# Fused chunk attention and snake MLP: k and q of batch 1 as fp32 through SyncE's queue, whole-width transposes, and a new order of work

## The chip, the cores and the metric

The kernel runs on one NeuronCore of a Trainium2 chip. TensorE (PE), VectorE (DVE), ScalarE (ACT), GpSimd (POOL) and SyncE (SP) each work off their own instruction stream in order. They meet at semaphores. DMAs are issued from SP and ACT on one kind of queue and from POOL on another. The metric is the device time of one execution in microseconds; the median of three runs is compared.

## The reference

Four batches of 768 tokens, eight heads of 64. Each chunk of 32 queries attends to 8 memory keys and to its own 32 keys with 16 to the left and 8 to the right; the result, 3072 x 512, goes through a two-layer network with a sine between.

```python
for c in range(nc):                                  # chunks of 32 queries
    l_start, r_end = max(0, c_start - 16), min(S, c_end + 8)
    k_full = concatenate([mem_k, k[:, :, l_start:r_end]], axis=2)
    v_full = concatenate([mem_v, v[:, :, l_start:r_end]], axis=2)
    a = softmax(scale * q_c @ k_full.T)
    out[:, :, c_start:c_end] = a @ v_full
x = out.transpose(0, 2, 1, 3).reshape(B * S, H * D)
h = x @ w_in                                         # 512 -> 2048
s = sin(alpha * h)
g = h + s * s / (alpha + 1e-09)
return g @ w_out                                     # 2048 -> 512
```

## The kernel before, in words

The work goes batch by batch. A front (a `Stage` with index -1) does the attention of batch 0. Then four passes follow. Pass i does both layers of batch i and, inside it, the attention of batch i + 1, so that PE has something to do while the other engines work on a tile.

**Attention.** Queries are taken 96 at a time. Scores need k and q with the head dimension on the partitions. Batches 0 and 1 get them by PE: `turn` (L269) transposes one piece, that is two heads (a head pair, `hp`) of k or of q, in twelve transposes of 128 x 64, and `put_k` (L282) or `put_q` (L297) copies the result out of PSUM. Batches 2 and 3 use DMA transposes. `scores` and `u_scores` take the exponential on ACT. `values` and `u_values` multiply with v and, in `normed` (L350), divide by the row sums on DVE. `turned` (L362) turns the result on PE and writes it to `xT`.

**Where k and q come from.** Batch 0: eight loads of 384 KB in fp32 by SP (`load_f`, L707) into `kq_f`, cast on chip piece by piece (L653, word "a"). Batch 1: two loads of 768 KB by POOL (`load_one`, L154, words "dq108" and "dk108"), which cast on the way, so no engine casts. Batches 2 and 3: rows by POOL (L232, L238, L245).

**The network.** For each of 16 tiles of the hidden layer (`ft`): `half_tile` (L422) does two halves of four matmuls with 384 columns; `sine` (L435) on ACT; `squared` (L441) on ACT, DVE or POOL, as a letter says; `finish` (L449) on DVE writes `gT`. The second layer (`second`, L458) has 96 matmuls of 512 columns a batch, which `feed` gives out in portions.

**The order is written out by hand.** Strings of words are read from left to right, and each word issues instructions. "b4" and "h4" are the two halves of tile 4, "q4V" its square on DVE, "g4" its end; "k0" and "l0" transpose the pieces of k and q for head pair 0, "K0V" and "L0A" copy them out on DVE and ACT; "a0V" casts piece 0 (0 to 3 are k, 4 to 7 q); "s", "v", "t"/"T"/"c" are scores, values and turns; "f7" gives out seven second-layer matmuls. Words that issue POOL DMAs: "V024" loads v of batch 0, heads 2 and 3 (`load_v`, L160, two DMAs, three for the first heads); "I02" loads `w_in` for tiles 0 and 1 (`load_w_in`, L212); "U56" loads `w_out` for tile 5; "dm" loads the memory values. "C" words make constants: "Cp", "Cz", "Cv", "Cs" and "Ci" on POOL. Each engine keeps the order of the words for its own instructions, POOL's DMA issues included, and waits where data is late.

In the front, POOL's order before is: Cp, Cz, Cv, Ci, dm, V024, V002, V068, V046, Cs, I02, I27; then from pass 0 I7g, U69, U12, dq108, dk108, Ufg, U01, U56. The first tile of batch 0 is b0, which needs I02 and the first half of `xT`.

Of the kernel before, what the change touches and what calls it, by code (L numbers as in the profile page):

```python
# [85 lines left out]
def kernel(  # L86
# [182 lines left out]
    def turn(src, hp):  # L269
        bank, bs = banks.single()  # L270
        t = bank[:, 0:384].bitcast(BF).rearrange("p (r c) -> p r c", r=6)
        for r in range(6):
            for e in range(2):
                nc.tensor.transpose(
                    t[64 * e:64 * e + 64, r, :], src[:, 2 * hp + e, r, :], ident[:]
                )
# [226 lines left out]
    class Stage:  # L503
# [146 lines left out]
        def do_a(self, a):  # L650
            hp = int(a[0]) % HP
            dst = kq[int(a[0]) // HP]
            copier(a[1])(  # L653
                dst[:, 2 * hp:2 * hp + 2].rearrange("p h r d -> p h (r d)"), kq_f[int(a[0])][:]
            )
# [7 lines left out]
        def do_d(self, a):  # L663
            if a == "m":
                nc.gpsimd.dma_start(memv_st[64:72].rearrange("n b h d -> n (b h) d"),
                                    mem_v.rearrange("b h n d -> n (b h) d"))
# [206 lines left out]
```

## Time and profile before

| What | Value |
|---|---|
| Median of three runs | 216.53 us (216.51 to 219.29) |
| Profiled execution: span from first to last instruction | 213.1 us |
| Median less span | 3.4 us |
| PE busy | 201.7 us, 95% of the span |
| ACT, DVE, POOL busy | 143.5, 140.5, 99.8 us |
| First of the 512 first-layer matmuls | 24.81 us |
| Granted clock of TensorE | 1.000 |

No time of its own is listed for the profiled execution beside the span, so the median less the span stands in for what lies around it. In the rows below, a row by stretches gives the stretch, its length, then busy time and instructions of each engine, the granted clock, the DMA share and GB/s. A row by time gives start, duration, engine, line, operation, tiles, shape and count; in brackets stands how long the engine sat idle before, and what ended that. A row of a DMA queue gives packets, MB and the share of 16 engines, which can pass 100% as packets overlap. A DMA's row gives issuer, count, size and microseconds from issue to landing.

### The profile page before, as it was taken

Reading aid. Unit: us, or ns where it says so; the run is one execution under the profiler, and the core shown is the slowest. Engines: PE = TensorE matmul, PEld = TensorE weight load, DVE = VectorE, ACT = ScalarE, POOL = GpSimd, SP = SyncE. Lnnn points to the kernel's source line nnn. Section 1 sums busy time; section 2 is a strip of 40 time slices with the busy share of each in tenths; the row PEclk is TensorE's granted clock in tenths of the full one; section 3 lists DMA queues with packets and bytes.
Section 4 is the critical chain, followed back from the end, with each engine's and each line's share of the span. In section 5 each row is a group of like instructions: output and inputs, shape, how many; then the busy total and the mean of one; then the engine's idle time right before and its main releaser. Section 6 shows DMA issues by size and latency. Waiting matters only on the chain.

```text
span 213.1 us, 4479 instructions
## 1 busy us (share of the span) xinstructions
PE 201.7 (95%) x1721; PEld 113.5 (53%) x1721; DVE 140.5 (66%) x218; ACT 143.5 (67%) x230; POOL 99.8 (47%) x140
## 2 busy tenths in 40 slices
PE   0799899999999999999999999999999999999994
PEld 0456555565455556555455555554555555554443
DVE  7598678999542749975856649898157197865011
ACT  2597898976857469977846199887846289891110
POOL 8959515688598193009991039659400023200000
PEclk9999999999999999999999999999999999999999
DMA  6999999999999999969999229989945400000312
GB/s 195 337 163 141 193 209 205 204 163 182 131 177 141 137 148 144 180 88 110 126 217 171 72 63 131 156 126 129 175 115 123 124 15 0 2 3 0 148 49 98
DMA packets 95908, 28.19 MB, mean 132 GB/s; under 512 B 84864, under 2 KB 92432, under 8 KB 95888
## 3 DMA queue, kind: packets, MB, share of 16 engines
q0 software_dynamic: 68736, 13.25, 92.3%
q1 hardware_dynamic: 26976, 14.62, 28.2%
q8 instruction: 13, 0.21, 0.4%
q14 instruction: 7, 0.06, 0.1%
q10 hardware_dynamic: 176, 0.04, 0.1%
HBM read 29.66 MB, written 6.29 MB: 169 GB/s over the span
## 4 chain that ended last, share of the span: by engine, by line
PE 71%; DVE 9%; DMA 7%; ACT 4%; issue 4%; POOL 3%; DVEq 0%; POOLq 0%; ACTq 0%
PE ps L462 38%; PE ps L424 27%; DMA memv_st<-in_mem_v_dram 4%; DVE gT L451 4%; DVE s L447 3%; DMA vw<-in_v_dram 3%; PE ps L414 3%; PE ps L385 2%; ACT u L439 2%; PE ps L366 1%; ACT s L444 1%; POOL s L447 1%; POOL vw L172 1%; DVE kT L285 1%; ACT L699 1%
## 5 line engine op out<-in xcount | busy, mean ns | idle before, releaser
L462 PE MATMUL ps<-w_out_sb,gT 128*128 128x512 bf16 (+2 forms) x400 | 89.1, 371 | 0.0
L424 PE MATMUL ps<-xT,w_in_sb 128*128 128x384 bf16 x512 | 86.0, 326 | 0.7 <-DVE gT L451 0.4
L451 DVE SCALAR_TENSOR_TENSOR gT<-s,inv_alpha,ps 128x768 bf16<-128x768 f32 x64 | 63.0, 1011 | 12.5 <-ACT s L444 5.2
L424 PEld LDWEIGHTS <-w_in_sb 128*128 128x128 bf16 x512 | 49.8, 98 | 35.4 <-issue 2.1
L439 ACT ACTIVATE u<-ps,alpha_sb 128x768 f32<-128x768 f32 x64 | 56.6, 895 | 16.8 <-PE ps L424 14.3
L462 PEld LDWEIGHTS <-gT 128*128 128x128 bf16 x400 | 36.6, 98 | 37.9 <-DVE gT L451 0.2
L447 POOL TENSOR_TENSOR s<-u 128x768 f32<-128x768 f32 x11 | 17.4, 1582 | 69.7 <-ACT u L439 69.7
L399 ACT ACTIVATE pt<-ps,biasm 128x256 bf16<-128x256 f32 x72 | 27.2, 489 | 10.5 <-PE ps L385 10.5
L469 DVE COPY o_sb<-ps 128x512 f32<-128x512 f32 (+1 forms) x15 | 10.1, 678 | 28.3 <-PE ps L462 26.4
L447 DVE TENSOR_TENSOR s<-u 128x768 f32<-128x768 f32 x23 | 21.9, 953 | 7.8 <-ACT u L439 7.8
L444 ACT ACTIVATE s<-u 128x768 f32<-128x768 f32 x30 | 25.0, 841 | 0.5
L354 DVE TENSOR_TENSOR x_blk<-ps,rinv 96x512 bf16<-96x512 f32 x32 | 22.0, 687 | 1.1
L469 ACT COPY o_sb<-ps 128x512 f32<-128x512 f32 (+1 forms) x10 | 5.6, 562 | 21.6 <-PE ps L462 21.6
L172 POOL DMA_DIRECT2D vw<-in_v_dram x13 | 12.9, 994 | 7.9 <-PE ps L366 5.4
L353 DVE RECIPROCAL rinv<-ps 96x8 f32<-96x8 f32 x32 | 6.4, 200 | 13.5 <-PE ps L414 12.7
L179 POOL DMA_DIRECT2D vw<-in_v_dram x13 | 12.7, 976 | 0.0
L238 POOL DMA_DIRECT2D kst<-in_k_dram x16 | 12.2, 760 | 1.1 <-DMA vw<-in_v_dram 0.8
L232 POOL DMA_DIRECT2D kst<-in_k_dram x16 | 11.3, 708 | 2.3 <-DMA vw<-in_v_dram 1.6
L369 ACT COPY xT<-ps 128x384 bf16<-128x384 bf16 x12 | 5.6, 496 | 8.2 <-PE ps L366 8.2
L245 POOL DMA_DIRECT2D q_bf<-in_q_dram x12 | 10.7, 912 | 0.0
L414 PEld LDWEIGHTS <-pt 128*128 128x128 bf16 x192 | 8.2, 97 | 4.2 <-ACT pt L399 0.3
L414 PE MATMUL ps<-vw,pt 128*128 128x65 bf16 x192 | 8.9, 193 | 0.0
(81 smaller groups left out, 131.4 us busy)
## 6 DMA issues: line engine op xcount, KB each, us to landing
out_dram<-o_sb SPq DMA_DIRECT2D x23, 256.0 KB, 2.3
kq_f<-in_k_dram SPq DMA_DIRECT2D x4, 384.0 KB, 6.5
kq_f<-in_q_dram SPq DMA_DIRECT2D x4, 384.0 KB, 6.0
q_bf<-in_q_dram POOLq DMA_DIRECT2D x12, 128.0 KB, 6.7
w_in_sb<-in_moe_w_in_dram POOLq DMA_DIRECT2D x1, 1152.0 KB, 12.6
vw<-in_v_dram POOLq DMA_DIRECT2D x7, 128.0 KB, 6.7
vw<-in_v_dram POOLq DMA_DIRECT2D x8, 112.0 KB, 7.4
kst<-in_k_dram POOLq DMA_DIRECT2D x14, 64.0 KB, 5.1
```

The lines of the kernel that those rows point to most:

```text
L172: nc.gpsimd.dma_start(vw[0:64, lo:c1, 0:D], win(vflat, a, n, 64))
L179: nc.gpsimd.dma_start(vw[72:128, c0:hi, 0:D], win(vflat, base + QW * c0 + 48, hi - c0, 56))
L354: nc.vector.tensor_tensor(out=x_blk[:].rearrange("p g e d -> p e g d"), in0=otv[0:QW, :, :, 0:D], in1=rinv[:].unsqueeze(3).to_broadcast([Q ...
L399: nc.scalar.activation(pt[:, 0:H * QW].rearrange("p (g e c) -> p g e c", g=2, e=4)[:, :, :, 32 * m:32 * m + 32], sc[:, :, 0:4 * QW].rearra ...
L414: nc.tensor.matmul(otv[:, e, hp, :], pt[:, QW * i:QW * i + P], vws[b % 2][:, 2 * hp + e, j, 0:D + 1],)
L424: nc.tensor.matmul(t["hT"][:, hf, 0:HALF], w_in_sb[:, kt, P * t["ft"]:P * t["ft"] + P], t["xT"][:, kt, HALF * hf:HALF * hf + HALF], start= ...
L439: nc.scalar.activation(t["u"][:], t["hT"][:, :, 0:HALF], ACTF.Sin, scale=alpha_sb[:, ft:ft + 1])
L444: nc.scalar.activation(s2[:], u[:], ACTF.Square)
L447: e.tensor_tensor(out=s2[:], in0=u[:], in1=u[:], op=ALU.mult)
L451: nc.vector.scalar_tensor_tensor(out=gT[:, ft, :].rearrange("p (e c) -> p e c", e=2), in0=t["s2"][:], scalar=inv_alpha[:, ft:ft + 1], in1= ...
L462: nc.tensor.matmul(o[:, c0:c1], gT[:, ft, P * s:P * s + P], w_out_sb[:, ft, c0:c1], start=(ft == 0), stop=(ft == FT - 1),)
L469: copier(state["engines"][state["o"] % len(state["engines"])])(o_sb[:, c0:c1], o[:, c0:c1])
```

## The change

1. The two POOL loads of k and q for batch 1 go. Instead SP loads eight fp32 pieces of 384 KB into a new buffer `kq_1` (word "j": "jkP0123" and "jqP0123" in pass 0). A small memset on POOL stands ahead of each four; the loads wait for it. `kq_1` takes one of the two buffers of `gT`.
2. Eight casts for batch 1 in pass 0: "a7P", "a6P", "a0P", "a1P" on POOL, "a4V", "a2V", "a3V" on DVE, "a5A" on ACT. The casts of batch 0 may stand on POOL too: "a0P" and "a2P" in the front.
3. The casts write the two heads of a piece side by side, so that `turn` needs six transposes of 128 x 128 instead of twelve of 128 x 64.
4. All five strings are new. In the front POOL's order becomes: Ci, a0P, Cz, dm, Cv, V002, a2P, V024, V046, Cp, V068, Cs, I27, I02; then in pass 0 I7g, the memset for k, U69, U12, U01, U24, Ufg, the memset for q, the square of tile 6, that of tile 7, a6P, a7P, U56, U45. The second-layer portions are mostly smaller ("f16" becomes "f12 f1" and the like); there are 96 matmuls a batch as before.

```diff
+FRONT = (
+    'Cb a1A Ci Cm a4V a0P k0 a5A z4 l0 Cz K0V Cl We dm Cv k1 V002 Ck L0A l1 K1A a3V L1A a6A a7V a2P s00 '
+    's01 k2 l2 m0 K2A s10 V024 V046 eVA s11 z4 k3 Cp L2V v10 l3 V068 K3A L3A Cs I27 s20 v11 v01 s30 v00 '
+    'z1 s31 v30 s21 T01 v31 T10 v20 T00 eVA T30 v21 z1 T31 z1 t20 t11 I02 t21 Ws '
+)
+PASSES = ((
+    'o8 b0 I7g jkP0123 h0 b1 U69 h1 U12 b4 q0V q1A g0 h4 b3 h3 g1 q4V q3A g4 U01 b6 b2 h2 U24 Ufg h6 b5 '
+    'h5 jqP0123 g3 b7 q6P q2V h7 q7P a6P q5A g2 a7P U56 a4V b10 g6 g5 h10 b9 q10A h9 b8 h8 g7 q8A g10 q9V '
+    'a2V b11 h11 g9 b13 g8 U45 h13 l0 q11V l2 l3 k2 a0P L0A L2A V158 q13A g11 g13 K2A a1P b15 h15 Uef '
+    'q15V b12 Ube g15 h12 q12A U9b a5A b14 V102 V125 g12 h14 q14P f7 k0 k1 l1 a3V L3A k3 K1V L1V K3A f4 '
+    'f1 f3 f2 f3 K0A s61 g14 f12 f1 s70 f1 f8 s3 f1 f1 m1 v6 v0 f1 f1 f1 f7 v3 f3 f2 t0 f1 s542 f1 f5 f4 '
+    'T3 f1 v1 f1 f1 f2 v4 v2 f2 f3 Ws c4 v7 f1 c6 c2 f1 t1 f1 f1 v5 f2 f3 f4 f1 T7 f2 f1 f1 T5 f5 '
...
-    k_bf = consts.tile([P, H, 6, D], BF, name="k_bf")
-    q_bf = consts.tile([P, H, 6, D], BF, name="q_bf")
+    k_bf = consts.tile([P, HP, 6, 2, D], BF, name="k_bf")
+    q_bf = consts.tile([P, HP, 6, 2, D], BF, name="q_bf")
...
-    def load_one(src, dst, b, h0, h1):
-        nc.gpsimd.dma_start(
-            dst[:, h0:h1].rearrange("p h r d -> p h (r d)"),
-            src[b, h0:h1].rearrange("h (p r) d -> p h (r d)", p=P),
-        )
...
         for r in range(6):
-            for e in range(2):
-                nc.tensor.transpose(
-                    t[64 * e:64 * e + 64, r, :], src[:, 2 * hp + e, r, :], ident[:]
-                )
+            nc.tensor.transpose(
+                t[:, r, :], src[:, hp, r].rearrange("p e d -> p (e d)"), ident[:]
+            )
...
-            copier(a[1])(
-                dst[:, 2 * hp:2 * hp + 2].rearrange("p h r d -> p h (r d)"), kq_f[int(a[0])][:]
-            )
+            copy = nc.gpsimd.tensor_copy if a[1] == "P" else copier(a[1])
+            copy(dst[:, hp].rearrange("p r e d -> p e r d"),
+                 kq_f[int(a[0])].rearrange("p e (r d) -> p e r d", r=6))
...
+        def do_j(self, a):
+            x0 = 0 if a[0] == "k" else HP
+            hps = [int(c) for c in a[2:]]
+            eng = {"V": nc.vector, "P": nc.gpsimd}[a[1]]
+            for hp in hps:
+                kq_f[x0 + hp] = kq_1[:, x0 + hp]
+            eng.memset(kq_1[0:1, x0 + hps[0]:x0 + hps[-1] + 1, 0, 0:1], 0.0)
+            for hp in hps:
+                load_f(k if x0 == 0 else q, hp, kq_f[x0 + hp], 1)
...
+    kq_1 = gp.tile([P, 2 * HP, 2, 6 * D], F32, name="kq_1", tag="gT")
...
-    stage.run((
-        'a1A Cb Cp Cz Cv a5A eVA Cm Cl z4 a0V Ci k0 dm a4V l0 k1 K0V Ck l1 L0A V024 We L1V a2A K1A V002 '
-        'a6V k2 s00 K2V a3V s11 V068 m0 a7V s01 l2 s10 k3 K3A L2A V046 z4 v10 l3 Cs L3A I02 v11 s20 z1 '
-        'v01 s30 z1 v00 s31 z1 v30 s21 v31 T01 T10 v20 T30 T00 v21 T20 T31 I27 t11 t21 eVA Ws '
-    ))
-    for i, words in enumerate(((
-        'o8 b0 h0 I7g q0V U69 U12 b1 h1 dq108 q1A b4 h4 b3 g0 h3 b6 g1 dk108 q4V g4 q3A b2 h2 h6 b5 h5 '
-        'Ufg g3 b7 q2V U01 U56 q6P h7 g2 q5A b10 U24 q7P g6 h10 b9 q10A g5 h9 U45 b8 h8 g7 g10 q8A q9V '
-        'V158 b11 h11 g9 b13 g8 h13 l0 l2 l3 L0A L2A q13P k2 q11V Ube b15 U9b g11 Uef g13 K2V h15 b12 '
-        'q15V h12 q12A b14 g15 f7 h14 V125 k1 k0 g12 l1 K1V k3 L1V L3A q14V K3A K0A V102 f9 g14 s61 f16 '
-        'm1 s70 s3 f13 v0 f3 v6 c6 f6 v3 f5 s542 T3 f10 T0 v4 f6 v2 f2 v1 c4 c2 f7 v7 f1 T1 f3 v5 Ws T7 '
-        'f8 t5 '
...
+    stage.run(FRONT)
+    for i, words in enumerate(PASSES):
```

The strings of passes 1 to 3 are new in the same manner: the same tiles, squares, scores, values and loads in another order, with smaller portions.

More of the change, by code (lines that the diff above doesn't have):

```diff
@@ L18 @@
 ALU = mybir.AluOpType
+FRONT = (
[3 rows of a table added]
+)
+PASSES = ((
[6 rows of a table added]
+), (
[5 rows of a table added]
+), (
[5 rows of a table added]
+), (
[3 rows of a table added]
+))
 class Feed:
@@ L138 @@
     kst = consts.tile([P, NJ, H * D], BF, name="kst")
-    k_bf = consts.tile([P, H, 6, D], BF, name="k_bf")
-    q_bf = consts.tile([P, H, 6, D], BF, name="q_bf")
-    qst = q_bf[:].rearrange("p h r d -> p (h r d)").rearrange("p (t c) -> p t c", t=NSUB)
+    k_bf = consts.tile([P, HP, 6, 2, D], BF, name="k_bf")
+    q_bf = consts.tile([P, HP, 6, 2, D], BF, name="q_bf")
+    qst = q_bf[:].rearrange("p g r e d -> p (g r e d)").rearrange("p (t c) -> p t c", t=NSUB)
     NK = NM * sum(not CROSSED[b][0] for b in range(B))
@@ L672, in do_d @@
                             mem_k[bb].rearrange("h n d -> n h d"))
-            else:
-                src, dst = (k, k_bf) if a[0] == "k" else (q, q_bf)
-                load_one(src, dst, int(a[1]), int(a[2]), int(a[3]))
+        def do_j(self, a):
[7 more added lines that the diff above has]
+                load_f(k if x0 == 0 else q, hp, kq_f[x0 + hp], 1)
         def do_I(self, a):
@@ L699, in warm, with load_f @@
         nc.scalar.activation(tiny[:], zeros[0:1, 0:1], func)
-    kq_f = [mlp.tile([P, 2, 6 * D], F32, name="kq_f", tag=t) for t in ("u", "s2") * 4]
+    kq_f = [mlp.tile([P, 2, 6 * D], F32, name="kq_f", tag=t)[:] for t in ("u", "s2") * 4]
+    kq_1 = gp.tile([P, 2 * HP, 2, 6 * D], F32, name="kq_1", tag="gT")
     memk_f = mlp.tile([P, H, D], F32, name="memk_f", tag="o_sb", bufs=3)
     alpha_rows = mlp.tile([FT, P], F32, name="alpha_rows", tag="o_sb", bufs=3)
-    def load_f(src, hp, t):
+    def load_f(src, hp, t, b=0):
         nc.sync.dma_start(
-            t[:], src[0, 2 * hp:2 * hp + 2].rearrange("h (p r) d -> p h (r d)", p=P)
+            t, src[b, 2 * hp:2 * hp + 2].rearrange("h (p r) d -> p h (r d)", p=P)
         )
@@ L812 @@
     stage.tile = first
-    stage.run((
[3 rows of a table removed]
-    ))
-    for i, words in enumerate(((
[6 rows of a table removed]
-    ),(
[5 rows of a table removed]
-    ),(
[5 rows of a table removed]
-    ),(
[3 rows of a table removed]
-    ))):
+    stage.run(FRONT)
+    for i, words in enumerate(PASSES):
         stage = Stage(i, stage.nx).run(words)
```

26 rows, old and new, of tables (PASSES, stage) are left out of this document.

## The prediction

> **What bounds the kernel now.** I read the page's totals first, then the busy time by stretches, then the front in order of time, then the DMA queues by window.
>
> ```profile
> span 213.1 us, 4479 instructions
> PE 201.7 (95%) x1721; PEld 113.5 (53%) x1721; DVE 140.5 (66%) x218; ACT 143.5 (67%) x230; POOL 99.8 (47%) x140
> ```
> ```profile
> 24.00:28.00 4.00, 3.85 (x36) 2.47 (x33) 1.87 (x4) 3.51 (x6) 1.03 (x2) 1.00 1.14 213
> 28.00:36.00 8.00, 7.83 (x48) 4.48 (x46) 7.01 (x9) 6.86 (x9) 1.82 (x2) 1.00 1.21 206
> 36.00:44.00 8.00, 7.99 (x88) 5.14 (x87) 7.49 (x8) 7.85 (x11) 5.17 (x6) 1.00 1.28 205
> 44.00:54.00 10.00, 9.69 (x105) 5.50 (x106) 9.54 (x14) 6.86 (x10) 9.08 (x12) 1.00 1.91 166
> 190.00:213.10 23.10, 20.24 (x110) 9.96 (x108) 5.67 (x7) 4.10 (x7) 0.00 (x0) 1.00 0.18 69
> 28.00:213.10 185.10, 181.36 (x1414) 100.13 (x1411) 119.87 (x163) 124.84 (x203) 78.24 (x89) 1.00 1.13 121
> ```
> The first number after the length is PE's busy time, then PEld, DVE, ACT, POOL. From 28 us to the end PE lacks 185.1 - 181.4 = 3.7 us, of which 23.1 - 20.2 = 2.9 us is the tail behind its last matmul. So between 28 us and the tail only 0.8 us is idle. Two things set the time: the moment at which the first-layer matmuls of batch 0 begin, and the amount of PE work behind it. The span stands 3.4 us under the median of the runs (216.5); I add every change to that median.
>
> The front decides the first of the two:
>
> ```profile
> 4.86 0.90 POOL L665 DMA_DIRECT2D memv_st<-in_mem_v_dram  x1
> 6.57 1.12 POOL L179 DMA_DIRECT2D vw<-in_v_dram  x1
> 14.34 1.76 POOL L172 DMA_DIRECT2D vw<-in_v_dram  x1 [2.52 <-DMA memv_st<-in_mem_v_dram]
> 16.09 0.88 POOL L179 DMA_DIRECT2D vw<-in_v_dram  x1
> 18.03 2.27 POOL L213 DMA_DIRECT2D w_in_sb<-in_moe_w_in_dram  x3
> 27.01 0.54 POOL L219 DMA_DIRECT2D w_out_sb<-in_moe_w_out_dram  x1 [2.52 <-DMA w_in_sb<-in_moe_w_in_dram]
> ```
> ```profile
> 16.11 0.41 PE L344 MATMUL ps<-vw,pt 128*128 128x65 bf16 x8
> 22.29 0.42 PE L344 MATMUL ps<-vw,pt 128*128 128x65 bf16 x8 [0.25 <-DMA vw<-in_v_dram]
> 24.81 17.62 PE L424 MATMUL ps<-xT,w_in_sb 128*128 128x384 bf16 x104
> ```
> ```profile
> w_in_sb<-in_moe_w_in_dram POOLq DMA_DIRECT2D x1, 256.0 KB, 4.6
> w_in_sb<-in_moe_w_in_dram POOLq DMA_DIRECT2D x1, 640.0 KB, 7.9
> ```
> Two waits of POOL show a rule of its queue. The ninth DMA (14.34) waited for the first to land, the twentieth (27.01) for the twelfth, the 640 KB of w_in: eight are in flight. The two w_in pieces landed at 18.03 + 4.6 = 22.6 and at 27.0, in the order of issue. The first value matmuls went at 16.1 and the last v load released PE at 22.3: six full-sized v loads and one tiny one in 6.2 us, about 1 us each. POOL's queue works its loads off one behind the other, and the first layer, at 24.8, followed close on them.
>
> **The change part by part.**
>
> *The w_in pieces change places.* In the new front "I27" (640 KB, columns of first-layer tiles 2 to 6) stands ahead of "I02" (256 KB, tiles 0 and 1), and the first tile is still b0. The columns of b0 now land behind everything that had landed at 27.0 before: the same v loads and the same two pieces. POOL also has a cast, "a0P", ahead of its first load; it waits for k's first piece. So the memory load goes out near 6 us, not at 4.9. That costs little, since POOL's queue moved nothing so early anyhow:
>
> ```profile
> q1 hardware_dynamic: 909, 1.32, 100.1%
> ```
> ```profile
> q1 hardware_dynamic: 198, 0.29, 95.3%
> q0 software_dynamic: 195, 0.01, 25.0%
> ```
> ```profile
> q0 software_dynamic: 560, 0.78, 114.0%
> ```
> ```profile
> q0 software_dynamic: 4318, 0.52, 369.6%
> ```
> ```profile
> q0 software_dynamic: 787, 0.09, 72.5%
> q1 hardware_dynamic: 249, 0.45, 64.2%
> ```
> These are the queues (packets, MB, share) in five windows: 5 to 9 us, SyncE's queue alone; 10 to 11, both; 22 to 26, POOL's queue alone with w_in; 14 to 18, the same with v; 59 to 61, both, with k rows and stores. In the first the two quoted loads of POOL were out, and none of their packets moved. So the floor for b0 is 27.0, against 24.8: +2.2 us.
>
> *K and q of batch 1 go to SyncE's queue.* POOL loses two issues and gains a tiny memset, behind its third w_in issue; eight loads of 384 KB then follow on SP, four at that memset and four at a second one. I estimate when, from POOL's rows and k's first load:
>
> ```profile
> kq_f<-in_k_dram SPq DMA_DIRECT2D x1, 384.0 KB, 3.9
> ```
> That load, issued in the first microsecond, takes 3.9 to land, so the cast ends near 5.5; the memory load and seven v issues of about 0.9, the second POOL cast and the memsets bring POOL to some 15, the last two v issues to 17, two memsets to 18, and three w_in issues in 2.27 to 20.1; SyncE's first bytes follow near 21.5. At that time the last w_in data are still to come. Taking some 2 us from data to landing (a store of the page's list lands in 2.3), data ran until 25.0: 3.5 us of POOL's queue are left at 21.5. A packet takes 16 engines x 4 us / 909 = 70 ns on SyncE's queue, 16 x 4 / 560 = 114 ns for w_in. Dealt one for one, as the equal counts of 10 to 11 us say (198 and 195), POOL's queue keeps 114 / 184 = 62%: 3.5 / 0.62 = 5.6 us, so b0's columns land at 21.5 + 5.6 + 2.0 = 29.1. The bounds are 27.0 (no contention) and, with POOL's queue at the 35% of its bytes that 59 to 61 shows (0.09 / 2 = 0.045 MB/us, where v alone moves 0.52 / 4 = 0.13), 21.5 + 10 + 2 = 33.5. I take 29.0, since w_in has long packets, and those of 59 to 61 are short. The Trainium skill, "DMA: Bandwidth & Descriptors", section "Queues, rings and completion order", says that each DMA engine goes round robin between its queues, a whole packet at a time. By that rule the landing is the 29.1 of the sum, by the byte shares 33.5; the equal counts at 10 to 11 us agree with it, 787 to 249 at 59 to 61 does not, and 909 to none at 5 to 9 does not either.
>
> *The value chain of the front.* The loads of heads 6 and 7 are now the last; four value groups need or follow them, where two did. Each has a reciprocal and a scaling on DVE:
>
> ```profile
> L354 DVE TENSOR_TENSOR x_blk<-ps,rinv 96x512 bf16<-96x512 f32 x32 | 22.0, 687 | 1.1
> L353 DVE RECIPROCAL rinv<-ps 96x8 f32<-96x8 f32 x32 | 6.4, 200 | 13.5 <-PE ps L414 12.7
> ```
> Two more at 0.89 put the first layer at 24.8 + 1.8 = 26.6, under the 29.0 of the weights: hidden by that wait, and worth 1.8 us if it were gone. The casts and transposes that come earlier in the front are hidden by the v loads: at nothing, with 16.1 as their due time.
>
> *Six transposes a piece.* Twelve halves become six whole ones.
>
> ```profile
> 42.30:44.00 1.70, 1.63 (x48) 1.45 (x48) 1.00 1.23 202
> 49.60:51.20 1.60, 1.52 (x48) 1.37 (x48) 1.00 1.27 212
> ```
> ```profile
> L462 PE MATMUL ps<-w_out_sb,gT 128*128 128x128 bf16 x16 | 1.1, 219 | 0.0
> ```
> Batch 1's 96 take 1.63 + 1.52 = 3.15 us, 33 ns each: halves already overlap in pairs. A whole one has 128 columns at full width. By the first-layer row 17.62 / 104 = 169 ns for 384 columns, so 56 ns; by the row above 1.1 / 16 = 69 ns. 48 of them cost 2.7 to 3.3 us: between 0.45 less and 0.15 more. I take 0.4 less, as back to back is the nearer case. In batch 0 it lies ahead of the v loads and counts nothing.
>
> *Eight casts more.* Four on POOL, three on DVE, one on ACT.
>
> ```profile
> L653 DVE CAST q_bf<-kq_f 128x768 bf16<-128x768 f32 x3 | 2.2, 728 | 0.0
> L653 ACT CAST q_bf<-kq_f 128x768 bf16<-128x768 f32 x1 | 0.8, 832 | 0.2 <-DMA kq_f<-in_q_dram 0.2
> L760 POOL COPY mind<-asum 128x768 bf16<-128x768 bf16 x1 | 0.8, 815 | 0.0
> L447 DVE TENSOR_TENSOR s<-u 128x768 f32<-128x768 f32 x23 | 21.9, 953 | 7.8 <-ACT u L439 7.8
> L444 ACT ACTIVATE s<-u 128x768 f32<-128x768 f32 x30 | 25.0, 841 | 0.5
> L285 DVE COPY kT<-ps 128x672 bf16<-128x672 bf16 x4 | 3.4, 853 | 0.9 <-PE ps L274 0.9
> ```
> DVE gains 3 x 0.73 and gives away one square (0.95) and one k copy (0.85): +0.4. ACT gains the cast (0.83), that square (0.84) and that copy (at its cast's rate 0.83 at most): +2.5. In the stretch 28 to 54 DVE is busy 7.01 + 7.49 + 9.54 = 24.0 of 26 us and ACT 21.6; ACT's rises to 24.1. Both still fit, so I take nothing; with no slack the two would cost at most 2.9. POOL's four (0.82 each, bounded above by the time for which q is late) stand ahead of w_out issues; see the rivals.
>
> *Order and smaller portions in batches 1 to 3.* PE has 0.8 us to win in all, so I take 0.2 off. The cover is second-layer work; where it ran out, at least a tile's sine and square would be exposed, 0.9 + 0.95 us at a time:
>
> ```profile
> L439 ACT ACTIVATE u<-ps,alpha_sb 128x768 f32<-128x768 f32 x64 | 56.6, 895 | 16.8 <-PE ps L424 14.3
> ```
>
> Sum: 216.5 + 4.2 - 0.4 - 0.2 = **220.1 us**.
>
> **The rivals.**
> 1. *POOL's queue is crowded out.* With the 35% above, b0 begins at 33.5: 216.5 + 8.7 - 0.6 = 224.6. The blank POOL queue at 5 to 9 us speaks for it, the long packets of w_in against. It makes the kernel over 2% slower as soon as b0 begins later than 24.8 + 4.3 + 0.6 = 29.7.
> 2. *POOL blocks on q.* "a6P" and "a7P" wait on POOL for the last q pieces. Eight pieces of 384 KB (3.1 MB) at 38% of SyncE's 1.32 / 4 = 0.33 MB/us take up to 25 us, until 46, and the w_out issues of tiles 4 and 5 stand behind them on POOL. The second layer starts here before the change:
>
> ```profile
> 47.43 1.67 PE L462 MATMUL ps<-w_out_sb,gT 128*128 128x512 bf16 x7
> ```
> It would be due near 47.4 + 4.2 = 51.6. If q lands after 48, these loads stop PE; at 50 it costs some 2: 222.1.
> 3. *No contention.* SyncE's loads come later or POOL's keep their rate: b0 at 27.0, 218.1.
> 4. *Faster.* b0's columns do not hang on the 640 KB (the pieces travel side by side) and the value chain closes as early as before: 24.8, and PE wins 0.4 and the 0.8 idle: 215.3. Against it stand the landings in the order of issue. Over 2% faster would need b0 before 22, ahead of the last v load.
>
> **How the numbers follow.** Forecast 43% (218.8 to 221.2), rival 1 17%, rival 2 10%, rival 3 20%, rival 4 10%. Two per cent, about what a measurement of this kernel tells from no change, is 4.3 us: 212.2 to 220.9. Slower: all of rival 1, nearly all of rival 2, and about 0.13 of the forecast, whose upper end passes 220.9: 39%. Faster: 4%, from the far end of rival 4. The same: 57%. The range leaves out the lower part of rival 4 and the upper part of rival 1: 216.2 to 224.2.
>
> **What would show it.** In the changed profile, the first L424 matmul near 29 and waiting on w_in; the 256 KB load landing behind the 640 KB one; SyncE's eight 384 KB loads beside w_in from 21.5; 48 transposes near 2.75 us; PE full from there to the tail. The prediction is wrong if the first layer starts by 25, if PE waits for a cast, or if PE has new gaps of over 1 us behind 54 us.

## The result and the profile after

The changed kernel takes 233.84 us (median; 233.25 to 235.8), the kernel before 216.52 beside it: a ratio of 1.0835, interval [1.0769, 1.0902]. 220.1 was forecast. Times here are medians of all executions, while ratios leave out disturbed ones (over 1.5% above the fastest of the same kernel), as are the profiles of E1, E12 and E15 and all of E1's times but 227.8 us.

The page of the changed kernel: the span, PE's row, and the two lines of the chain that ended last.

```profile
span 231.6 us, 4322 instructions
PE 206.8 (89%) x1625; PEld 115.5 (50%) x1625; DVE 142.1 (61%) x219; ACT 144.3 (62%) x230; POOL 103.1 (45%) x147
...
PE 49%; DMA 21%; POOL 10%; ACT 7%; issue 6%; DVE 6%; SPq 1%; DVEq 0%; ACTq 0%
PE ps L484 29%; PE ps L446 15%; DMA kq<-in_q_dram 8%; ACT u L461 5%; DMA q_bf<-in_q_dram 4%; DVE gT L473 3%; DMA kT<-kst 3%; PE ps L436 2%; DMA xT<-x_blk 2%; POOL vw L202 2%; PE ps L407 2%; POOL vw L195 2%; DMA kq_f<-in_k_dram 2%; DVE s L469 2%; POOL w_out_sb L242 1%
```

Three things that the prediction's sum did not price stand in the chain: the new q loads (8%), the row loads of q in the later batches (4%) and the DMA transposes of k (3%). To place them I cut both spans at the first first-layer matmul of each pass. First the kernel before, then the changed one; columns as in the prediction's rows by stretches (stretch, length, PE, PEld, DVE, ACT, POOL, granted clock, DMA, GB/s).

```profile
24.81:75.48 50.67, 50.17 (x472) 28.57 (x470) 35.52 (x52) 38.23 (x63) 30.66 (x38) 1.00 1.60 174
75.48:122.06 46.58, 46.57 (x376) 25.71 (x374) 33.48 (x48) 32.60 (x57) 22.30 (x27) 1.00 1.56 139
122.06:168.14 46.08, 45.92 (x357) 25.00 (x355) 30.04 (x42) 34.04 (x57) 21.37 (x23) 1.00 1.16 122
168.14:213.10 44.96, 41.88 (x241) 22.80 (x239) 21.88 (x24) 22.83 (x30) 4.44 (x3) 1.00 0.13 48
```
```profile
28.56:83.82 55.26, 51.90 (x420) 29.12 (x421) 37.27 (x53) 38.80 (x63) 35.13 (x43) 0.97 1.43 170
83.82:133.40 49.58, 47.28 (x372) 25.92 (x372) 34.13 (x48) 31.42 (x56) 19.51 (x24) 1.00 1.26 128
133.40:184.76 51.36, 47.43 (x357) 25.45 (x354) 28.98 (x41) 35.21 (x58) 21.20 (x24) 0.97 1.11 108
184.76:231.60 46.84, 42.23 (x241) 22.62 (x239) 23.61 (x25) 21.27 (x28) 6.09 (x4) 1.00 0.14 49
```

| | before | after | difference | of it PE idle |
|---|---|---|---|---|
| first first-layer matmul | 24.81 | 28.56 | +3.75 | |
| pass 0 | 50.67 | 55.26 | +4.6 | +2.9 |
| pass 1 | 46.58 | 49.58 | +3.0 | +2.3 |
| pass 2 | 46.08 | 51.36 | +5.3 | +3.8 |
| pass 3 | 44.96 | 46.84 | +1.9 | +1.5 |

PE idle is length less busy. In passes 0 and 2 the rest is busy time too long, and the clock column says why: 0.97. The front costs about what was forecast. The other 14.7 us lie where the forecast had 0.6 to win.

The front and pass 0 on PE, and the two other engines that matter there:

```profile
28.56 10.71 PE L446 MATMUL ps<-xT,w_in_sb 128*128 128x384 bf16 x64 [2.18 <-DMA w_in_sb<-in_moe_w_in_dram]
...
43.14 7.04 PE L446 MATMUL ps<-xT,w_in_sb 128*128 128x384 bf16 x32 [2.26 <-DVE gT L473]
...
55.80 1.67 PE L484 MATMUL ps<-w_out_sb,gT 128*128 128x512 bf16 x7
```
```profile
40.75 1.41 DVE L676 CAST q_bf<-kq 128x768 bf16<-128x768 f32 x1 [1.39 <-DMA kq<-in_q_dram]
42.08 3.77 DVE L473 SCALAR_TENSOR_TENSOR gT<-s,inv_alpha,ps 128x768 bf16<-128x768 f32 x4
```
```profile
45.50 0.82 POOL L676 CAST q_bf<-kq 128x768 bf16<-128x768 f32 x1 [3.76 <-DMA kq<-in_q_dram]
46.86 1.08 POOL L676 CAST q_bf<-kq 128x768 bf16<-128x768 f32 x1 [0.53 <-DMA kq<-in_q_dram]
47.89 1.14 POOL L242 DMA_DIRECT2D w_out_sb<-in_moe_w_out_dram  x2
```
```profile
44.00:48.00 4.00, 4.00 (x17) 1.95 (x15) 3.56 (x5) 1.24 (x2) 1.96 (x3) 0.61 0.25 84
```
The first layer waits for w_in, as forecast. Then DVE reaches its cast of q's first piece (word "a4V") before the piece is there, waits 1.39 us and takes 1.41 for it. Four "finish" steps queue behind it; they free the PSUM banks that PE needs, and PE stands 2.26 us. For the next 4 us the granted clock is 0.61, and 17 matmuls take the 4.00 us in which 24 of 169 ns would fit. POOL waits 3.76 us for another piece of q, and the next w_out issue goes out at 47.89.

### The profile page after: what moved, and what is told of

Its sections match the earlier page's. It is cut to its first block, busy times and chain, and to the rows that moved or that the text cites. A ratio compares the mean times of both kernels' runs of the same rounds, so it can differ in the third digit from the quotient of the medians.

```text
span 231.6 us, 4322 instructions
## 1 busy us (share of the span) xinstructions
PE 206.8 (89%) x1625; PEld 115.5 (50%) x1625; DVE 142.1 (61%) x219; ACT 144.3 (62%) x230; POOL 103.1 (45%) x147
## 4 chain that ended last, share of the span: by engine, by line
PE 49%; DMA 21%; POOL 10%; ACT 7%; issue 6%; DVE 6%; SPq 1%; DVEq 0%; ACTq 0%
PE ps L484 29%; PE ps L446 15%; DMA kq<-in_q_dram 8%; ACT u L461 5%; DMA q_bf<-in_q_dram 4%; DVE gT L473 3%; DMA kT<-kst 3%; PE ps L436 2%; DMA xT<-x_blk 2%; POOL vw L202 2%; PE ps L407 2%; POOL vw L195 2%; DMA kq_f<-in_k_dram 2%; DVE s L469 2%; POOL w_out_sb L242 1%
## 5 line engine op out<-in xcount | busy, mean ns | idle before, releaser
L446 PE MATMUL ps<-xT,w_in_sb 128*128 128x384 bf16 x512 | 87.7, 330 | 7.0 <-DVE gT L473 2.4
L484 PE MATMUL ps<-w_out_sb,gT 128*128 128x512 bf16 (+2 forms) x400 | 91.4, 374 | 0.4 <-DVE gT L473 0.4
L469 POOL TENSOR_TENSOR s<-u 128x768 f32<-128x768 f32 x12 | 18.6, 1552 | 93.2 <-ACT u L461 79.8
L469 DVE TENSOR_TENSOR s<-u 128x768 f32<-128x768 f32 x23 | 22.6, 983 | 17.0 <-ACT u L461 17.0
L491 DVE COPY o_sb<-ps 128x512 f32<-128x512 f32 (+1 forms) x15 | 10.1, 679 | 30.7 <-PE ps L484 30.6
L466 ACT ACTIVATE s<-u 128x768 f32<-128x768 f32 x29 | 24.5, 843 | 0.8
L195 POOL DMA_DIRECT2D vw<-in_v_dram x13 | 11.9, 916 | 3.9 <-PE ps L436 3.9
L202 POOL DMA_DIRECT2D vw<-in_v_dram x13 | 13.0, 1004 | 0.0
L407 PE MATMUL ps<-qT,kT 64*128 64x96 bf16 x192 | 6.7, 207 | 4.3 <-DMA qT<-q_bf 3.8
L391 ACT COPY xT<-ps 128x384 bf16<-128x384 bf16 x10 | 4.7, 486 | 8.9 <-PE ps L388 8.9
```

Of the source, the lines that this page charges most:

```text
L195: nc.gpsimd.dma_start(vw[0:64, lo:c1, 0:D], win(vflat, a, n, 64))
L202: nc.gpsimd.dma_start(vw[72:128, c0:hi, 0:D], win(vflat, base + QW * c0 + 48, hi - c0, 56))
L446: nc.tensor.matmul(t["hT"][:, hf, 0:HALF], w_in_sb[:, kt, P * t["ft"]:P * t["ft"] + P], t["xT"][:, kt, HALF * hf:HALF * hf + HALF], start= ...
L466: nc.scalar.activation(s2[:], u[:], ACTF.Square)
L469: e.tensor_tensor(out=s2[:], in0=u[:], in1=u[:], op=ALU.mult)
L484: nc.tensor.matmul(o[:, c0:c1], gT[:, ft, P * s:P * s + P], w_out_sb[:, ft, c0:c1], start=(ft == 0), stop=(ft == FT - 1),)
```

## The experiments

Each is cut into passes in the same way; "lengths" are the passes 0 to 3 of its profiled execution.

**Which strings cost what.** E1 is the changed kernel with the strings of passes 1 to 3 of the kernel before; E2 is the kernel before with the new strings 1 to 3.

```diff
 E1:  FRONT, PASSES[0] new
-     PASSES[1:4] new
+     PASSES[1:4] as before
 E2:  front, pass 0, k and q by POOL as before
-     strings 1 to 3 as before
+     strings 1 to 3 new
```


> The changed kernel with the strings of passes 1 to 3 from before. Theory: the 10.4 us that the changed profile loses in passes 1 (3.1) and 2 (7.3) come from the strings of these passes themselves; then 233.8 - 10.4 = 223.4 us, within 1.5. Rival: these losses are handed on from pass 0, where POOL is late with its loads; then the old strings lose them too, and the time stays over 229.

> The kernel before with the new strings of passes 1 to 3 and nothing else of the change. Theory (the strings lose the time themselves): 216.5 + 10.2 = 226.7 us, within 1.5. Rival (handed on from pass 0): 216 to 219.

E1: 233.05 us (227.8 to 233.98), start 28.9 us, lengths 57.0, 53.1, 46.1, 45.7. E2: 224.67 us, ratio 1.0403 [1.0333, 1.0474], lengths 50.7, 48.3, 53.2, 45.7. So pass 2's loss belongs to its own new string: the old one gives 46.1 behind the changed pass 0, the new one 53.2 behind the old pass 0. Pass 1 is another matter. The new string costs 1.7 us on the kernel before, but the old string, behind the changed pass 0, costs 6.5 (E5, below, has 6.7). Something is handed on from pass 0.

**Pass 2.** E6, E10 and E13 are E2 with a few words moved. E6 gives pass 1 back one portion of 14 and loads the last piece of q ahead of the square of tile 14. E10 keeps the portion, takes that load back to its place and puts the fourth q load ahead of the v load V305 instead. E13 is E10 with V305 behind the square of tile 14. E14 is the kernel before with one word moved.

```diff
 E6, pass 1:   - s05 V202 f1 f1 f1 v2 f1 f4 v1 f4 v4 f4 f2 f1 c4   + s05 V202 f14 v2 f1 v1 f1 v4 f2 f1 c4
 E6, pass 2:   - b15 q14P X8 h15 f2 f1 q15A R1 f2                  + b15 R1 q14P X8 h15 f2 f1 q15A f2
 E10, pass 2:  - h11 V305 g7 R1 q11A                               + h11 R1 V305 g7 q11A
 E13, pass 2:  - h11 V305 g7 R1 q11A .. q14P X8                    + h11 R1 g7 q11A .. q14P V305 X8
 E14, pass 2 of before:  - q9P b10 .. q13P X3 V305 h12             + q9P V305 b10 .. q13P X3 h12
```


> The kernel before with the new strings of passes 1 to 3 (224.7 us), and two edits: in pass 1 fourteen second-layer matmuls stand in one portion between the scores of blocks 0 and 5 and the first values, instead of three; in pass 2 the last load of q is issued ahead of tile 14's square on POOL instead of behind it. Theory: pass 1 goes from 48.2 to 46.6 us, since PE no longer runs dry while ACT takes the exponentials, and pass 2 from 53.2 to 46 to 47, since the last transposed q lands 3 us earlier: 216 to 217.5 us in all. Rivals: pass 1 stays at 48, bound by ACT; pass 2 stays over 50, bound by the DMA transposes themselves.

> The kernel before with the new strings of batches 1 to 3 (224.7 us), with pass 1's three portions between the first scores and the first values made one again (47.6 us in the run that had this, 46.6 before), and in pass 2 one R1 put ahead of V305 instead of behind g7, so that four loads of q for batch 3 stand ahead of the v load, as in the kernel before, and not three. Theory A (pass 2's loss of 7 us is that one load of 128 KB: behind the v load it lands some 9 us later, the transposes and the scores wait for it, and PE has nothing else): pass 2 goes from 53-54 to 46-48 us and the time to 217-219. Theory B (the portions of one or two and the later places of the squares make it): pass 2 stays at 51-54 us and the time at 223-225.

> The run with the q load ahead of the v load (224.9 us, pass 2 54.1), and V305 put behind the square of tile 14 on POOL (q14P), so that these 600 KB are issued some 23 us after the pass's start and not 16.9. Theory A (the v load collides with the four transposes of q: 9.6 us from issue to landing in place of 3.3; scores and PE wait): the transposes land within 4.5 us of their issue, no wait of PE for them over 1 us, pass 2 is 46-48.5 us and the time 217-219.5; the values may wait up to 1 us for v. Theory B (the portions of one or two and the places of the squares): pass 2 stays above 51 us, time 222-225.

> The kernel before with all its strings, and in pass 2 one word moved: V305 from behind the square of tile 13 (issued 20.2 us after the pass's start) to behind that of tile 9 (about 15 us), all four q loads still ahead of it. Theory A (as above): the four transposes of q take 7 to 11 us from issue to landing, PE waits 3 to 7 us for them and is throttled behind that, pass 2 goes from 46.1 to 50-54 us and the time to 220-225. Theory B (the new string's portions and squares are the cause): pass 2 stays within 1 us of 46.1 and the time within 1 us of before.

| | median, us | ratio | pass 1 | pass 2 |
|---|---|---|---|---|
| E6 | 224.41 | 1.0335 [1.0228, 1.0442] | 47.6 | 54.0 |
| E10 | 224.94 | 1.0436 [1.0362, 1.0509] | 47.6 | 54.1 |
| E13 | 218.76 | 1.0158 [1.0078, 1.0239] | 47.6 | 47.4 |
| E14 | 222.62 | 1.0302 [1.0231, 1.0373] | 46.5 | 53.4 |

My first theory, a q load that stands too late, fell with E6 and E10. The rows of E10 showed another cause. POOL's issues and the scores in the kernel before, E10, E13 and E14, in this order:

```profile
129.55 3.53 POOL L245 DMA_DIRECT2D q_bf<-in_q_dram  x4
...
142.23 1.28 POOL L172 DMA_DIRECT2D vw<-in_v_dram  x1
```
```profile
138.52 1.82 POOL L245 DMA_DIRECT2D q_bf<-in_q_dram  x2
140.31 1.25 POOL L172 DMA_DIRECT2D vw<-in_v_dram  x1
```
```profile
152.86 0.34 PE L385 MATMUL ps<-qT,kT 64*128 64x96 bf16 x8 [3.09 <-DMA qT<-q_bf]
155.69 0.50 PE L385 MATMUL ps<-qT,kT 64*128 64x96 bf16 x8 [2.48 <-DMA qT<-q_bf]
```
```profile
138.42 2.69 POOL L245 DMA_DIRECT2D q_bf<-in_q_dram  x3
...
147.13 1.27 POOL L172 DMA_DIRECT2D vw<-in_v_dram  x1
```
```profile
150.42 0.34 PE L385 MATMUL ps<-qT,kT 64*128 64x96 bf16 x8 [2.93 <-DMA qT<-q_bf]
152.42 0.51 PE L385 MATMUL ps<-qT,kT 64*128 64x96 bf16 x8 [1.66 <-DMA qT<-q_bf]
```
The four transposes of q on SyncE's queue start some 15.5 us after the pass's start in the kernel before and in E10. The v load (600 KB in two issues) follows 4.7 us behind the first of them in the kernel before, and 1.4 in E10. From issue to landing, by the page's column, the transposes take:

```profile
qT<-q_bf SPq DMA_TRANSPOSE x4, 3.3
```
```profile
qT<-q_bf SPq DMA_TRANSPOSE x4, 9.6
```
(before, then E10). In the changed kernel the v load goes out 0.4 us behind the first of these transposes. They take 7.0, and PE waits 3.8 us for them:

```profile
qT<-q_bf SPq DMA_TRANSPOSE x4, 7.0
```
```profile
160.86 0.34 PE L407 MATMUL ps<-qT,kT 64*128 64x96 bf16 x8 [1.13 <-DMA qT<-q_bf]
163.84 0.51 PE L407 MATMUL ps<-qT,kT 64*128 64x96 bf16 x8 [2.63 <-DMA qT<-q_bf]
```
E14 puts the v load 15.1 us after the pass's start, the last of the four q loads issued 5 us earlier, with the old portions and the old squares: the transposes take 9.3 us, PE waits 4.6, and the pass loses 7.3. E13 puts it 23.8 us after the start and gets 6.7 us back; PE's wait for q falls from 5.6 to 0.7. So the v load beside the transposes of q is the main cause, and portions and squares are not; the 1.3 us by which E13's pass 2 is still too long were not traced. My 4.5 us for E13's transposes was missed: the median is 6.5, with two q loads of 128 KB beside them, but they were through in time. The mended portion of 14 returned 0.65 of pass 1's 1.7 us.

**Pass 1.** The loads for batch 3's v are freed by batch 1's values at the end of pass 0, and the 64 KB of memory rows of k ("Z") follow the last output stores on SyncE's queue. Eight transposes of k wait for them, six of q for those, then the scores. E5 has q first in pass 0 (E4, below) and old strings 1 to 3. E11 is E5 with a small copy on POOL (word "Y") that reads the memory rows, so that the v loads and four q loads ("R4", moved ahead of them) go out behind the rows.

```diff
 E5:   - I7g jkP0123 .. h5 jqP0123      + I7g jqP0123 .. h5 jkP0123     (and strings 1 to 3 as before)
 E11, pass 1:  - R3 V378 b11 h11 b10 g9 V226 h10 R4    + R3 Y R4 V378 b11 h11 b10 g9 V226 h10
+        def do_Y(self, a):
+            nc.gpsimd.tensor_copy(held[64:72], kst[64:72, NJ - 1])
```


> The changed kernel with q loaded ahead of k for batch 1 and with the strings of passes 1 to 3 from before. The run with the old strings alone still needed 53.1 us for pass 1 (46.6 before), with the old string in it. Theory: that is handed on by pass 0, where POOL stands at the casts of q and issues the loads for pass 1 late; with q early POOL is early, pass 1 takes 46.6 to 48 and pass 2 46.1, and the time is near 220.5 us (219.5 to 222). Rival: pass 1 is slow with the new pass 0 for another reason; it takes 50 to 53 again, and the time is 224 to 227.

> The changed kernel with q loaded first and the old strings of batches 1 to 3 (230.3 us, pass 1 53.2 us), and in pass 1 a small copy on POOL that reads the memory rows of kst, ahead of the four q loads and of V378 and V226, so that these 1.1 MB are issued only when the 64 KB of memory rows have landed. Theory A (pass 1's loss, handed on from pass 0: the memory rows leave SyncE's queue 4.6 us after V378 and not 2.7, stand beside the v and q loads and take 7.9 us and not 4.2; eight transposes of k, six of q and then the scores follow one behind the other): the rows land within 3.5 us, the first scores come 4 to 5 us earlier against the pass's start, pass 1 is 47-49 us and the time 224.5-226.5. Theory B (the late output stores ahead of the rows on SyncE, or the q loads, set it): pass 1 stays at 51-54 us, or the q transposes now wait for q.

E5: 230.33 us, ratio 1.0503 [1.0343, 1.0662], lengths 53.7, 53.2, 46.2, 46.1. E11: 224.11 us, ratio 1.0361 [1.0263, 1.0459], lengths 53.3, 47.0, 46.1, 45.7. SyncE's rows before, in E5, in E11:

```profile
76.54 0.91 SPq L253 DMA_DIRECT2D kst<-memv_st  x1
80.76 10.73 SPq L260 DMA_TRANSPOSE kT<-kst  x8
```
```profile
82.08 0.91 SPq L281 DMA_DIRECT2D kst<-memv_st  x1
89.97 10.93 SPq L288 DMA_TRANSPOSE kT<-kst  x8
```
```profile
85.22 0.91 SPq L282 DMA_DIRECT2D kst<-memv_st  x1
88.69 11.54 SPq L289 DMA_TRANSPOSE kT<-kst  x8
```
Read the step from the first row to the second: 4.2 us before, 7.9 in E5, 8.7 in the changed kernel (84.49 to 93.16), 3.5 in E11. PE's wait for qT in pass 1 falls from 3.8 us in E5 to 0.3 in E11, and the pass from 53.2 to 47.0. The margin is thin: the v loads now run beside the transposes of q, and E18 (below), with the same string, waits 2.1 us for qT and takes 48.8. E5's own theory, that POOL's lateness through its casts is handed on, was wrong: q first took that lateness away, and pass 1 did not gain.

**The front.** E3 gives the changed kernel the small piece of w_in first; E9 gives the kernel before nothing but the exchange.

```diff
 E3:  - Cs I27 s20 .. t11 I02 t21     + Cs I02 s20 .. t11 I27 t21
 E9:  - L3A I02 v11 .. T31 I27 t11    + L3A I27 v11 .. T31 I02 t11
```


> The changed kernel, with only the two pieces of w_in in the front exchanged: the 256 KB for tiles 0 and 1 ahead of the 640 KB. Both theories: the first L446 matmul moves from 28.6 to about 26.2, where its x is ready. Theory A: the time behind it is then bound by the landing of q of batch 1 at 40.7, which does not move; the gain is used up there, and the time falls by under 1 us, to 233 or more. Theory B: what begins earlier ends earlier; it falls by 2.3 us, to 231.5.

> The kernel before with nothing of the change but the exchange of the two pieces of w_in: I27 (640 KB) takes I02's place and I02 (256 KB) the last. Theory A (the prediction's front term: the first pass's first matmul needs I02, POOL's queue serves its requests in turn, so I02 cannot land before the 640 KB ahead of it): the first first-layer matmul goes from 24.8 to 26.5-27.5 us, without any load of SyncE's beside it, and the time from 216.5 to 218-219.5, since PE is full from there to the tail. Theory B (the pieces run side by side, and the lateness of 3.75 us seen in the changed kernel is all of it the k loads' contention): 24.8 to 25.3 us at most, and the time within 0.7 us of before.

E3: 235.54 us, ratio 1.0883 [1.0783, 1.0983]; the first layer starts at 26.61 with no wait in brackets, right behind the last turn of x. E9: 219.12 us, ratio 1.0148 [1.0071, 1.0225]; start 28.15, pass 0 52.0 with the clock at 0.68 in its first 5 us (shown at the end), the later passes as before.

```profile
28.15 2.10 PE L424 MATMUL ps<-xT,w_in_sb 128*128 128x384 bf16 x6 [1.51 <-DMA w_in_sb<-in_moe_w_in_dram]
```
So the exchange makes the start 3.3 us later and the kernel 1.5% slower, without any load of SyncE's beside it. The small piece lands behind the large one (28.1 and 25.6 us): the pieces do not run side by side. But 1.0 of the 3.3 us is not the exchange: POOL waited longer for earlier loads in this execution, and w_in went out at 18.99, not at 18.03.

What SyncE's loads add shows in the time from the first w_in issue to the landing of the second piece: 8.7 us in the kernel before, 9.1 in E9, 11.0 in the changed kernel. This time scatters. Seven profiles without SyncE's loads beside w_in (before, E2, E6, E9, E10, E13, E14) have 8.4 to 10.1, on average 9.1; seven with them and the large piece first (changed, E4, E5, E7, E8, E11, E18) have 8.7 to 12.0, on average 10.0. So the contention is some 1 us, less than the scatter.

In E3 the 2 us were more than used up by pass 0, 58.9 long: DVE waited 4.7 us for q and POOL 6.6, since q lands at its own time.

**Pass 0.** E4 exchanges q and k alone. E7 puts DVE's cast of q later. E12 is E11 with the small piece of w_in first. E15 is E11 with the w_out issues ahead of POOL's casts of k and DVE's cast of k's piece 2 later; E16 is E15 with the small piece first; E17 is E16, and E18 is E15, with the transposes of that piece 12 matmuls later still (the expectation counted 16).

```diff
 E4:   - I7g jkP0123 .. h5 jqP0123             + I7g jqP0123 .. h5 jkP0123
 E7:   - U56 a4V b10 .. U45 h13 l0             + U56 b10 .. U45 h13 a4V l0
 E12:  E11 with  - I27 s20 .. I02 t21          + I02 s20 .. I27 t21
 E15:  E11 with  - q9V a2V b11                 + q9V b11
                 - U45 h13 l0 .. l3 k2 a0P     + U45 Uef Ube U9b h13 l0 .. l3 a0P
                 - q13A g11 g13 K2A            + q13A g11 a2V g13 k2 K2A
 E17:  E16 with  - g13 k2 K2A a1P .. b12 g15   + g13 a1P .. b12 k2 K2A g15
```


> The changed kernel, with the two groups of SyncE's loads for batch 1 exchanged: q first, k at the second memset. The casts of q stand ahead of most casts of k. Theory: the waits of DVE (1.4 us at 40.7) and POOL (4.3 us to 46.8) for q go, PE's gap at 41 to 43 and its slow clock behind it with them; the first second-layer matmul moves from 55.8 to about 52, and the time falls by 3 to 4.5 us, to 229.3 to 230.8. Rival: k is then late instead, for the casts of k on DVE and POOL, and the time stays within 1 us of 233.8.

> The changed kernel with one cast moved: that of q's first piece on DVE stands ahead of the transposes that need it, not ahead of tile 10. The loads stay as they are. Theory: PE's gap at 41 to 43 and the slow clock behind it come from DVE standing at this cast; from the first L446 matmul to the first of pass 1 it takes 50.5 to 52 us instead of 55.3, and the time falls by 3 to 5 us. Rival: POOL's wait for the later pieces of q sets the end of pass 0; it stays over 54.

> The run before this one (q first, old strings of batches 1 to 3, memory rows ahead of the v loads) with I02 ahead of I27 as well. Theory A (what the change costs is its orders; its own idea, fp32 pieces by SyncE's queue and casts on chip, leaves a start later by some 1 us and a first pass longer by some 2): start 25.5-26.5 us, passes 51-53, 47-49, 46.1 and 45.9 us, time 219-222, so still not below the kernel before. Theory B (the earlier start is used up in the first pass again, as it was when I02 went first without q first): pass 0 is 54 us or more and the time stays within 1 us of the run before this one.

> The changed kernel with q first, the old strings of batches 1 to 3, the memory rows ahead of the v loads (224.1 us; start 30.8 in its profile, pass 0 53.3), and in pass 0 the four w_out issues Uef, Ube and U9b put right behind U45, ahead of POOL's casts of k, and VectorE's cast of k's piece 2 with its transposes some two tiles later. Theory A (what is left of pass 0's loss is VectorE standing at that cast, the activations gT behind it, PE's gap and the half clock after it): no PE wait of over 1 us in the first 30 us of pass 0, pass 0 50.5-52 us, time 221.5-223.5. Theory B (the fp32 traffic itself slows what pass 0 needs, or the transposes now come too late for the scores): pass 0 stays at 52.5-54.5 us, time within 1 us of 224.1.

> The run before this one with I02 ahead of I27. Theory A (the earlier start was used up by VectorE's late cast alone): start 26-27 us, pass 0 51-52.5, time 219.5-222. Theory B (the start is used up whatever the order, since q and k land at a time of their own): pass 0 is longer by what the start is earlier, 53.5 us or more, and the time stays within 1 us of the run before this one.

> The run with pass 0 mended and I02 first (222.7 us; start 27.3, pass 0 54.1 with a PE gap of 2.4 us and half clock behind it), and the six transposes of k's piece 2 put behind both halves of tile 15, 16 to 20 matmuls later. Theory A (the gap and its half clock are what is left of the loss): no PE gap over 1 us in pass 0, clock 1.0 throughout, pass 0 50.5-52 us, start 26.5-27.5, time 219-221. Theory B (PE runs out of other work wherever k's transposes stand, since the second layer's first portions and the scores stand behind them): the gap moves on, pass 0 stays at 53.5-55 us, time within 1 us of 222.7.

> The same with I27 ahead of I02, as in the changed kernel. Theory A (with no wait left in pass 0, a start later by 2 us is a time longer by 2 us): start 28.5-30 us, pass 0 as in the run before this one to 0.7 us, time 1.5-3 us above it. Theory B (q and k land at a time of their own and set the pass's end): pass 0 is shorter by what the start is later, the time within 1 us of the run before this one.

| | median, us | ratio | start | pass 0 | pass 1 | pass 2 | pass 3 |
|---|---|---|---|---|---|---|---|
| E4 | 230.16 | 1.0669 [1.0586, 1.0752] | 26.8 | 52.5 | 49.9 | 53.0 | 45.8 |
| E7 | 234.89 | 1.0841 [1.0732, 1.0950] | 29.1 | 57.0 | 49.4 | 52.8 | 46.4 |
| E12 | 224.38 | 1.0333 [1.0233, 1.0433] | 26.9 | 56.3 | 48.6 | 46.1 | 45.5 |
| E15 | 224.62 | 1.0318 [1.0213, 1.0423] | 30.1 | 55.4 | 46.6 | 46.1 | 45.2 |
| E16 | 222.71 | 1.0337 [1.0276, 1.0398] | 27.3 | 54.1 | 46.5 | 46.1 | 45.2 |
| E17 | 221.81 | 1.0308 [1.0268, 1.0348] | 27.2 | 51.4 | 46.5 | 46.1 | 46.7 |
| E18 | 224.07 | 1.0285 [1.0223, 1.0347] | 27.1 | 50.8 | 48.8 | 46.1 | 45.6 |

E4: no cast of q waits any more, and the kernel gains 3.7 us (in the profiles the start is 1.7 earlier and pass 0 2.7 shorter); a gap of 2.17 us stays, now behind DVE's cast of k. E7: DVE's wait goes, the time does not, since POOL still stands 3.84 us at its casts, and PE then waits 3.3 us for the w_out loads behind them. So the two waits are parallel: both must go. E15 and E16 missed: with the casts and w_out issues mended, PE waited for k's cast itself. The last rows of this set show the end of it, E16 and then E17, in time:

```profile
48.42 0.68 PE L302 MATMUL ps<-ident,k_bf 128*128 128x128 bf16 x6 [2.35 <-DVE k_bf L682]
```
```profile
45.00:50.00 5.00, 2.65 (x29) 1.97 (x27) 4.29 (x6) 3.85 (x6) 5.00 (x7) 0.86 1.22 227
50.00:55.00 5.00, 5.00 (x25) 2.59 (x25) 2.12 (x3) 2.63 (x4) 2.64 (x3) 0.80 2.89 149
```
```profile
45.00:50.00 5.00, 4.10 (x39) 2.61 (x37) 4.90 (x6) 4.32 (x6) 5.00 (x6) 1.00 1.21 233
50.00:55.00 5.00, 4.95 (x44) 3.19 (x43) 4.60 (x8) 4.80 (x8) 3.55 (x4) 1.00 2.73 155
```
In E17 no gap of PE in pass 0 is over 0.7 us, the clock stays at 1.00, and the pass is 51.4 us, in E18 50.8; 50.7 was before. So pass 0's loss is a matter of where waits stand and not of the fp32 traffic. E18 did not tell what the exchange costs behind a mended pass 0: its start was no later than E17's. With the large piece first, starts ran from 26.8 (E4) to 30.8 (E11), with the small one from 26.6 to 27.3 (E3, E12, E16, E17).

No version beats the kernel before. E17 keeps the idea of the change without its three collisions (casts that wait for loads, memory rows behind v loads, a v load beside the transposes of q) and is still 3.1% slower. In its profile the start is 2.3 us later than before, pass 0 0.7 longer and pass 3 1.8.

**Transposes.** E8 is the changed kernel with twelve halves a piece.

```diff
-            nc.tensor.transpose(t[:, r, :], src[:, hp, r].rearrange("p e d -> p (e d)"), ident[:])
+            for e in range(2):
+                nc.tensor.transpose(t[64 * e:64 * e + 64, r, :], src[:, hp, r, e], ident[:])
```


> The changed kernel with twelve transposes of half the width for each piece again, from the new layout. Theory: the halves overlap in pairs, so batch 1's take 3.1 to 3.2 us of PE in either form (3.15 before, 3.18 after) and the time stays within 1 us of the changed kernel's. Rival: the whole ones are cheaper by half, and the time rises by 1.5 us or more.

E8: 234.92 us, ratio 1.0815 [1.0714, 1.0915] against 1.0835 for six whole ones: no difference. Groups of the kernel before, then of the changed one (total busy us, mean ns):

```profile
L274 PE MATMUL ps<-ident,k_bf 128*64 128x128 bf16 x96 | 4.4, 235 | 0.1
L274 PE MATMUL ps<-ident,q_bf 128*64 128x128 bf16 x96 | 4.2, 233 | 0.0
```
```profile
L296 PE MATMUL ps<-ident,k_bf 128*128 128x128 bf16 x48 | 4.7, 250 | 3.9 <-DVE kT L313 1.9 <-POOL k_bf L676 1.6 <-DVE alpha_sb L816 0.3
L296 PE MATMUL ps<-ident,q_bf 128*128 128x128 bf16 x48 | 4.3, 242 | 0.3 <-ACT q_bf L676 0.3
```
For both batches 192 halves take 8.6 us and 96 whole ones 9.0.

## Why the prediction was wrong

**The front: right in size, in part by luck.** 4.2 us was forecast (2.2 for the order, 2.0 for contention), 3.75 came. The order of landing held, so rival 4 fell. In the profiled execution the parts are 1.9 for the order (second landing of w_in before, 26.7, less the start, 24.8), 2.3 for the longer way from issue to landing (11.0 against 8.7) and -0.5 for w_in going out at 17.5 and not at 18.0. Over the fourteen profiles the contention is only some 1 us, and SyncE's first packets moved behind 23.5 us, not at 21.5, so that the sum came so near is partly luck. Rival 3, no contention, fits some executions (8.7 us in E18) but not this one. One-for-one dealing held, and rival 1 fell with it. The queue rows of the changed kernel between 28 and 29 us:

```profile
q0 software_dynamic: 64, 0.14, 74.4%
q1 hardware_dynamic: 63, 0.10, 30.6%
```
The value chain was forecast to put the start at 26.6 if the weights were on time. E3 shows just that, 26.61, and E16 and E17 27.3 and 27.2. No run tests whether it is the two value groups.

**"Both still fit, so I take nothing" failed, in pass 0.** The sum added up busy time of DVE and ACT. It was not busy time that cost, but that a cast waits for a load at the head of an in-order engine. Rival 2 had this for POOL, with the right landing time ("up to 25 us, until 46"), and asked only whether w_out comes late. DVE's cast of q's first piece stands earlier, and what queues behind it frees PSUM; the prediction named nobody who waits behind it. Its cast also took 1.41 us, where 0.73 was taken. Measured: 4.6 us, of which 2.9 are idle, most of the rest a lowered clock. Shown by E4 and E7 together with E17 and E18, where the loss is gone (51.4 and 50.8 us with the same fp32 loads and casts).

**"PE has 0.8 us to win in all, so I take 0.2 off" failed, in passes 1 to 3.** This step priced the gain of the new order, and bounded its loss only by second-layer cover. It did not walk POOL's and SyncE's queues past each other. The new strings cost 9 us on the kernel before (E2). Of them 6.7 is one v load issued beside the transposes of q (E13 takes it away, E14 makes the like, 7.3, by that word alone). Behind the changed pass 0, pass 1 pays in addition for the memory rows behind the v loads (E5 against E11: 6.2 us with the old string). In the changed kernel as it stands, with the new string in pass 1, that pass lost 3.0; how much of it is the memory rows and how much the portions was not separated.

**"0.4 less" for the transposes failed in size:** nothing is saved. Batch 1's take 3.18 us on PE, where 3.15 stood before, within the bounds that were given.

**The chances hold a slip:** 0.13 of the forecast's 43% is 6%, so "slower" adds up to some 32%, not 39%.

**Open:** pass 3. It is 1.9 us longer in the changed kernel, and 0.7 to 1.8 longer in E5, E11, E17 and E18, although their strings 2 and 3 are those of the kernel before. Nearly all of it is one wait of PE for a DMA transpose into xT at the pass's start: 1.4 us in the changed kernel, 1.0, 0.6, 1.6 and 0.5 in the four; E16 has none there, and 45.2 us. Why this transpose comes late, no run isolates.

## What to carry to other kernels

Where PE is full, a new order has no gain to look for and every wait to fear: walk each moved DMA past the work of the other queue, and ask of each load what small or chained transfer will stand beside it. A cast that moves onto an engine can cost next to nothing when its data is there (E17, E18) and far more than its duration when it is late; look at what stands behind it on that engine and which buffers that frees. A wait mended alone may return little or nothing when a second one ends at the same time (E3, E7, E16): mend both before judging either.

## What the hardware showed beyond what was expected

PE's clock dropped after quite short gaps: 0.61 over 4 us behind 2.26 us of idle time in the changed kernel, 0.80 over 5 us behind 2.35 us in E16, and in E17, where no gap passes 0.7 us, 1.00. The stretch at the start of pass 0 shows that the gap's length is not all:

```profile
28.15:33.15 5.00, 5.00 (x22) 2.60 (x23) 0.96 (x1) 1.60 (x3) 0.53 (x1) 0.68 1.13 208
```
This is E9 behind a gap of 1.51 us; E18 had 1.40 us there and kept 1.00 between 25 and 35 us, and the changed kernel had 2.18 us there and kept 1.00 in its first 5 us. The Trainium skill, "TensorE: Matmul & The Clock Gate", section "What's actually happening", gives half clock after an idle window of some 3.4 us, and says that the window runs freely. The gaps here are shorter than that window; the measurement decides, and a free-running window fits the fact that like gaps ended differently.

A DMA transpose shares badly: beside 600 KB of v rows it took 9.3 to 9.6 us from issue to landing, without them 3.3 (E10, E14, before; medians). And the step behind 64 KB of memory rows inside SBUF was 3.5 us with no v load beside them (E11) and 7.9 to 8.7 behind v loads (E5, the changed kernel).
